# Recall in transposed layout, exp of phi from the copy on chip, and a newly searched plan, in a gated mix of attention with memory and a gated feed-forward layer

## The chip, the cores and the metric

The kernel runs on one core of one Trainium2 chip. The metric is device time in microseconds (us); lower is better. Every number of a run below is of a run in the fast state (one core, granted TensorE clock 0.993 to 1.000). The engines are called as the profile calls them: PE multiplies matrices, PEld loads its weights, DVE is the vector engine, ACT computes activations, POOL masks the attention here, and SP issues DMAs.

## The reference, cut to what matters

```python
def _A_ref(x, wq, wk, wv, wo, beta):         # S = 2048, D = 512, H = 32, Dh = 16, N = 4 segments of L = 512
    ...
    for s in range(N):
        qs, ks, vs = q[:, :, s], k[:, :, s], v[:, :, s]
        p = softmax(qs ks^T * scale + causal mask)
        a_dot = p vs
        pq = phi(qs)                          # phi(t) = t + 1 where t > 0, else exp(t)
        num = pq M                            # per head: 16 x 16 memory
        den = (pq z) + 1e-06
        o = g * num / den + (1 - g) * a_dot   # g = sigmoid(beta), one per head
        pk = phi(ks)
        M = M + pk^T vs
        z = z + sum(pk)
    return concat(o) @ wo

def _B_ref(x, W_gate, W_up, W_down):          # F = 1792
    gate = x @ W_gate
    return (relu(gate) * (x @ W_up)) @ W_down

x = A_x
g = sigmoid((x * gate_w).sum(-1))             # one per token
return g * _A_ref(x, ...) + (1 - g) * _B_ref(x, ...)
```

`pq M / den`, for all segments but the first, is called the recall.

## The kernel before

The kernel does not write its instructions in a fixed order. It describes tasks, each with an engine, an assumed duration, dependencies, a priority (`key`) and the PSUM banks and buffers that it needs, and then plays them through a list scheduler (`Plan`) while the program is built. The order in which tasks start in that play is the order of the program. A table `SHIFT` moves the priority of single tasks by their number; it is the result of a search. On the chip each engine keeps to its list: in the traces of the kernels before and after, the instructions of PE, DVE and ACT (2246 matmuls, 407 and 174 instructions in the changed kernel) start in exactly the program's order, compared by source line. A task may be marked `lock`: DVE and POOL tasks so marked are never planned at the same time.

```python
SHIFT = { 22: -80000, 23: 130000, ... }      # cut: 141 entries
...
    for t in sorted(ready, key=rank):        # in Plan.run
        ...
        if t.lock and busy["lock"] > now:
            continue
```

PSUM is the memory that matmuls write to. The plan divides it into eight banks; a fill of attention scores takes four, always the same, and the matmuls of everything else take whichever bank is free. Projections of Q and K land in a bank that two engines read, DVE for the copy in bf16 and ACT for the exp of phi:

```python
    def phi_exp(key, sl, a):
        es = plan.one("ex1")
        return es, plan.add("ACT", 478, key + 500, lambda: nc.scalar.activation(
            ex1[es.i][:], bank(sl), ACT.Exp), [a], ACL, need=[es], frees=[sl])
    ...  # proj_q: DVE casts bank(sl) to QT (frees=[sl] too); phi_exp(key, sl, a); DVE: pqT = phi(QT, ex1)
```

The recall puts heads in rows for the division: two matmuls per unit of eight heads, two banks, each flipped by DVE transposes into T (128x512 f32), then reciprocal, scaling and product there, and the product is flipped back with the attention result:

```python
    def recall(seg, c):
        for r in range(2):
            sl = work()
            a = plan.add("PE", 216, key + r, lambda r=r, sl=sl: nc.tensor.matmul(
                bank(sl), lhsT=mbd[i][:, c, r].rearrange("p j e -> p (j e)"), rhs=pqT[u % RQ][:],
                start=True, stop=True), [...], PEL, need=[sl])
            groups.append((sl, a))
        recalled[u] = normalise(u, 1, key, groups)   # 2 transposes, add, reciprocal, 2 products
```

The softmax here doesn't subtract the row's maximum and nothing guards it: scores larger than these inputs give would overflow.

## Time and profile before

277.18 us, median of three runs (277.01 to 277.35).

The head of the profile page: the span, each engine's busy time with its share and instruction count, and for PE and DVE the busy share in tenths of 40 equal slices.

```profile
span 275.4 us, 5541 instructions
PE 268.0 (97%) x2211; PEld 112.9 (41%) x2211; DVE 208.5 (76%) x457; ACT 195.5 (71%) x175; POOL 86.7 (31%) x139
PE   8999999989999999999999999999999999999995
DVE  5789788999999898598967992977998575464312
```

PE is busy everywhere. Because matmuls overlap (the profile gives each 128x512 one 380 ns), I also looked at starts: in an unbroken row, 128x512 matmuls start 216 ns apart. I call a hole whatever a start is later than is usual for its pair of shapes by over 0.12 us.

What the change touches, as groups of instructions (shape, count | busy us, mean ns of one | idle time just before them, and what ended it):

```profile
L657 DVE STREAM_TRANSPOSE T<-ps 128x512 f32<-128x512 f32 x56 | 37.1, 693 | 4.8 <-PE ps L626 4.3 <-PE ps L687 0.5
L511 ACT ACTIVATE ex<-ps 128x512 bf16<-128x512 f32 x24 | 14.3, 605 | 11.0 <-DVE ktr L538 8.9 <-DVE QT L522 1.2 <-PE ps L463 0.9
L687 PE MATMUL ps<-pqT,mbd 128*128 128x512 bf16 x24 | 8.1, 380 | 0.7 <-ACT ex L511 0.4
```

In the trace the two reads never overlap: of the 24 exps none runs at the same time as the cast of its bank, 18 come after it, and where one follows the other most closely the gap is 0.03 us. The casts in turn waited 1.1 us for exps. Why the two reads are kept apart, the trace doesn't show. One place where it costs PE something, from the chain of waits (start, length, what; all us):

```profile
92.66 0.65 DVE ktr L538
93.39 0.61 ACT ex L511
94.04 2.10 PE ps L463 x9
```

Cast, then exp, then the bank is free and PE goes on: the bank was held for 1.3 us from the start of the cast.

### The profile page before, as it was taken

The page shows a single profiled execution, that of the slowest core. Times are in us where ns is not written, and L with a number is a line of the kernel's source. Part 1 is how long each engine was busy: PE and PEld are TensorE (multiplying, and loading weights), DVE is VectorE, ACT ScalarE, POOL GpSimd, SP SyncE. Part 2 cuts the span into 40 slices and gives each one's busy share as a digit, 9 for nine tenths or more (in the row PEclk, how much of TensorE's full clock was granted, in tenths as well). Part 3 has the DMA queues.
Part 4 walks back from the last instruction along what each step waited for, and adds up shares of the span by engine and source line. Part 5 has one row for each costly group of instructions (what it writes and reads, how often), then busy time and mean ns, then how long its engine had stood idle before and what let it go on. Part 6 is the DMA issues. An engine that isn't in the chain of part 4 may idle for free.

```text
span 275.4 us, 5541 instructions
## 1 busy us (share of the span) xinstructions
PE 268.0 (97%) x2211; PEld 112.9 (41%) x2211; DVE 208.5 (76%) x457; ACT 195.5 (71%) x175; POOL 86.7 (31%) x139
## 2 busy tenths in 40 slices
PE   8999999989999999999999999999999999999995
PEld 4344344443434343433434444434343434444444
DVE  5789788999999898598967992977998575464312
ACT  2189899988887777988978779789878769333000
POOL 5023333324344253324242425243334342300000
PEclk9999999999999999999999999999999999999999
DMA  7999964022111120000000100000000010000011
GB/s 232 320 261 347 275 104 126 5 40 59 37 23 38 23 40 21 2 0 19 4 0 21 40 21 0 21 0 2 0 4 0 19 35 6 21 0 0 2 38 38
DMA packets 27993, 15.46 MB, mean 56 GB/s; under 512 B 15680, under 2 KB 27968, under 8 KB 27968
## 3 DMA queue, kind: packets, MB, share of 16 engines
q1 hardware_dynamic: 26752, 14.06, 19.7%
q10 hardware_dynamic: 1216, 1.06, 1.1%
q8 instruction: 17, 0.28, 0.5%
q14 instruction: 8, 0.07, 0.1%
HBM read 9.86 MB, written 2.10 MB: 43 GB/s over the span
## 4 chain that ended last, share of the span: by engine, by line
PE 84%; DVE 7%; ACT 4%; issue 2%; DMA 2%; SPq 0%; DVEq 0%; ACTq 0%
PE ps L463 65%; PE ps L584 8%; PE ps L626 7%; PE ps L687 2%; ACT ex L511 2%; ACT E L604 1%; DVE ktr L538 1%; PE ps L785 1%; ACT rgr L743 1%; DVE hT L749 1%; DMA ratio<-rcol 1%; DVE QT L522 1%; PE ps L480 1%; DVE pkT L506 1%; DMA rq<-ratio 1%
## 5 line engine op out<-in xcount | busy, mean ns | idle before, releaser
L604 ACT ACTIVATE E<-ps 128x2048 bf16<-128x2048 f32 x80 | 150.5, 1881 | 31.9 <-PE ps L584 26.2
L613 POOL TENSOR_SCALAR_AFFINE_SELECT E<-E 128x512 bf16<-128x512 bf16 x128 | 83.1, 664 | 150.8 <-ACT E L604 150.8
L463 PE MATMUL ps<-xT,wg_sb 128*128 128x512 bf16 x224 | 57.6, 380 | 0.1
L463 PE MATMUL ps<-xT,wu_sb 128*128 128x512 bf16 x224 | 57.2, 380 | 0.0
L463 PE MATMUL ps<-wd_sb,hT 128*128 128x512 bf16 (+1 forms) x238 | 54.5, 367 | 0.4 <-ACT ex L511 0.3
L749 DVE TENSOR_TENSOR hT<-ps,rgr 128x512 bf16<-128x512 f32 x56 | 37.8, 680 | 14.4 <-PE ps L463 9.3
L743 ACT ACTIVATE rgr<-ps 128x512 bf16<-128x512 f32 x56 | 32.1, 599 | 14.1 <-PE ps L463 13.8
L657 DVE STREAM_TRANSPOSE T<-ps 128x512 f32<-128x512 f32 x56 | 37.1, 693 | 4.8 <-PE ps L626 4.3
L463 PEld LDWEIGHTS <-hT 128*128 128x128 bf16 x238 | 21.6, 98 | 25.5 <-issue 5.4
L463 PEld LDWEIGHTS <-wu_sb 128*128 128x128 bf16 x224 | 20.4, 98 | 26.1 <-issue 4.3
L463 PEld LDWEIGHTS <-wg_sb 128*128 128x128 bf16 x224 | 20.3, 98 | 26.1 <-issue 4.7
L771 DVE TENSOR_SCALAR osr<-ps,ngcol 128x512 bf16<-128x512 f32 (+1 forms) x17 | 12.2, 719 | 24.4 <-PE ps L463 24.4
L511 ACT ACTIVATE ex<-ps 128x512 bf16<-128x512 f32 x24 | 14.3, 605 | 11.0 <-DVE ktr L538 8.9
L626 PE MATMUL ps<-E,Vp 128*17 128x256 bf16 (+3 forms) x512 | 20.6, 300 | 0.7 <-DVE hT L749 0.7
L662 DVE TENSOR_TENSOR och<-T,cfr 128x512 bf16<-128x512 f32 x28 | 20.4, 736 | 0.3
L584 PE MATMUL ps<-QT,KTe 32*128 32x512 bf16 (+3 forms) x256 | 17.3, 302 | 0.4 <-ACT E L604 0.4
L463 PE MATMUL ps<-wv_sb,xT 128*128 128x512 bf16 x64 | 17.0, 380 | 0.6 <-DVE grc L449 0.6
L463 PE MATMUL ps<-xT,wk_sb 128*128 128x512 bf16 x64 | 17.4, 380 | 0.1
L584 PE MATMUL ps<-QT,KTo 32*128 32x512 bf16 (+3 forms) x256 | 17.1, 299 | 0.1
L463 PE MATMUL ps<-xT,wq_sb 128*128 128x512 bf16 x64 | 16.6, 382 | 0.0
L463 PE MATMUL ps<-wo_sb,oT 128*128 128x512 bf16 (+1 forms) x68 | 16.6, 367 | 0.0
L626 PEld LDWEIGHTS <-Vp 128*17 128x17 bf16 x512 | 10.8, 91 | 13.2 <-issue 3.8
(70 smaller groups left out, 190.1 us busy)
## 6 DMA issues: line engine op xcount, KB each, us to landing
out_dram<-osr SPq DMA_DIRECT2D x15, 128.0 KB, 1.7
wd_sb<-in_B_W_down_dram SPq DMA_DIRECT2D x2, 896.0 KB, 10.1
xn<-in_A_x_dram SPq DMA_DIRECT2D x3, 512.0 KB, 3.9
wg_sb<-in_B_W_gate_dram SPq DMA_DIRECT2D x2, 512.0 KB, 9.2
wu_sb<-in_B_W_up_dram SPq DMA_DIRECT2D x2, 512.0 KB, 9.4
wg_sb<-in_B_W_gate_dram SPq DMA_DIRECT2D x2, 384.0 KB, 4.7
wu_sb<-in_B_W_up_dram SPq DMA_DIRECT2D x2, 384.0 KB, 5.3
wk_sb<-in_A_wk_dram SPq DMA_DIRECT2D x1, 512.0 KB, 7.3
```

The source lines that it names most:

```text
L463: nc.tensor.matmul(bank(sl)[:, 0:width], lhsT=lhsT, rhs=rhs, start=(start and q == 0), stop=(stop and q == n - 1))
L511: return es, plan.add("ACT", 478, key + 500, lambda: nc.scalar.activation(ex1[es.i][:], bank(sl), ACT.Exp), [a], ACL, need=[es], frees=[sl])
L584: nc.tensor.matmul(ps[:, j * L + off:j * L + off + n], lhsT=kt[32 * j:32 * j + 32, kb * P:(kb + 1) * P], rhs=QT[i][32 * j:32 * j + 32, kb ...
L604: nc.scalar.activation(Ef[:, e0 * L:e1 * L], ps[:, e0 * L:e1 * L], ACT.Exp, scale=SCALE),
L613: nc.gpsimd.affine_select(out=m, in_=m, compare_op=ALU.is_ge, fill=0.0, base=0, pattern=[[0, 4], [1, P]], channel_multiplier=-1)
L626: nc.tensor.matmul(bank(sl)[32 * j:32 * j + HW, kb * P:kb * P + w], lhsT=Vp[i][:, kb, 8 * c + 2 * j + r, 0:HW], rhs=E[(NFILL * u + f) % RE ...
L657: done.append(plan.add("DVE", 633, key - RL, lambda r=r, sl=sl: nc.vector.transpose(T[ts.i][:, r], bank(sl)), [a] + done, 60 if r else 0, ...
L662: nc.vector.tensor_tensor(och[ds.i].rearrange("p (q r e) -> p r q e", r=2, e=DH), t()[:, :, :, 0:DH], cfr[cs.i][:, :, :, None].to_broadcas ...
L687: a = plan.add("PE", 216, key + r, lambda r=r, sl=sl: nc.tensor.matmul(bank(sl), lhsT=mbd[i][:, c, r].rearrange("p j e -> p (j e)"), rhs=p ...
L743: r = plan.add("ACT", 478, key - RL, lambda sl=gsl, rs=rs: nc.scalar.activation(rgr[rs.i][:], bank(sl), ACT.Relu), [g], ACL, frees=[gsl])
L749: nc.vector.tensor_tensor(hT[hs1.i][:], bank(sl), rgr[rs.i][:], ALU.mult)),
L771: b = plan.add("DVE", 95 + 1.12 * w, key - RL, lambda: nc.vector.tensor_scalar(osr[os.i][:, 0:w], bank(sl)[:, 0:w], ngcol[:, tt:tt + 1], N ...
```

## The change

Intent: less work on PE and DVE in the recall, PSUM banks free sooner, and a plan searched anew. Four parts:

1. The recall's matmul is one per unit, and its result is already in the transposed layout that the output projection needs. The coefficient 1/den, times the token's part of the gate, is made by six small matmul groups (`dens`), in a layout of heads and tokens. It is written to DRAM and read back broadcast to 16 partitions per head; one DVE product applies it. The head's gate goes into the memory matrix itself.
2. The exps of phi read the bf16 copy that DVE made, not PSUM; the bank is free after the one cast.
3. `xn` has one buffer, not two, so that the load for segment 1 leaves the prologue.
4. The plan has a new rule (`GUARD`) and a new `SHIFT` table.

```diff
+GUARD = 0.0
 SHIFT = {
-    22: -80000, 23: 130000, 38: 50000, ...
+    34: 106376, 36: 113032, 40: -114448, ...        (177 entries)
 }
@@ in Plan.run
-                    if t.lock and busy["lock"] > now:
+                    if t.lock and (busy["lock"] > now or t.eng != "POOL" and any(
+                            p.lock and p.eng == "POOL" and now < p.avail < now + t.dur + GUARD
+                            for p in ready)):
                         continue
@@ phi
-    def phi_exp(key, sl, a):
+    def phi_exp(key, src, a):
         es = plan.one("ex1")
         return es, plan.add("ACT", 478, key + 500, lambda: nc.scalar.activation(
-            ex1[es.i][:], bank(sl), ACT.Exp), [a], ACL, need=[es], frees=[sl])
+            ex1[es.i][:], src(), ACT.Exp), [a], ACL, need=[es])
...
-            es, b = phi_exp(key, sl, a)
+            es, b = phi_exp(key, lambda: QT[i][:], prj["q", seg, c])
@@ the denominators, two per segment
+    def dens(seg, half):
+        ...
+                    nc.tensor.matmul(
+                        bank(sl)[32 * t:32 * t + 32, 0:P],
+                        lhsT=zbd[i][:, c].rearrange("p a h -> p (a h)"),
+                        rhs=pqT[(4 * seg + c) % RQ][:, t * P:(t + 1) * P], ...)
+        ... DVE: dnr = bank + 1e-6; dnr = 1 / dnr; dnr = dnr * rr
+        att["coefs", seg, half] = plan.add("SP", 360, key, lambda: nc.sync.dma_start(
+            out=coefs[n].rearrange("h t p -> t h p"), in_=dn()), [a], 2200, frees=[ds])
@@ the recall
+        b = plan.add("SP", 360, key - 3000, lambda: nc.sync.dma_start(
+            out=cdr[cs.i][:], in_=coefs[n][8 * k:8 * k + 8].rearrange("h t p -> h (t p)")[:, None]
+            .to_broadcast([8, 16, L])), [att["coefs", seg, c // 2]], 3800, need=[cs])
+        a = plan.add("PE", 216, key, lambda: nc.tensor.matmul(
+            bank(sl), lhsT=mbd[i][:, c].rearrange("p j r e -> p (j r e)"), rhs=pqT[u % RQ][:], ...)
+        a = plan.add("DVE", 605, key - RL, lambda: nc.vector.tensor_tensor(
+            omr[om.i][:], bank(sl), cdr[cs.i][:], ALU.mult), [a, b], DVL, need=[om], frees=[sl, cs])
(cut: buffers, the gate ratio in two forms, the memory matrices, adding omr to oT)
```

The new rule holds a locked DVE task back if a locked POOL task would become ready before the DVE task ended.

## The prediction

> **What bounds the kernel now.** TensorE. The page gives PE 97% busy (268.0 of 275.4 us), DVE 76%, ACT 71%, POOL 31%, clock full throughout. Busy matmul time proves little because matmuls overlap, so I took start-to-start distances from the timeline: back-to-back 128x512 matmuls start every 216 ns. [...] Each excursion to the attention tilings costs about 96 ns going in and 101 ns coming out (312 and 317 instead of 216). Beyond this there are only 16 larger holes after the first 5 us, together about 4.5 us: 1.1 us near 57 us, 1.0 near 29, and small ones around the recall matmuls (79, 93, 122, 155, 196-197 us), together about 2.1 us. The last 30 us are an unbroken row of L463 matmuls. The chain of waits agrees: PE 84%.
>
> **What the change does.**
> - PE: recall goes from 24 full matmuls (L687) to 12: -12 x 0.216 = -2.6 us. The six denominators (eight column-tiled matmuls of 128 columns each) add about 0.12 us each (estimate from the PV matmuls), linked behind a PV and thus without another tiling switch: +0.7 us. Net -1.9 us, all on the critical engine.
> - DVE: 24 of the 56 transposes T (693 ns) go: -16.6 us; 12 of 28 products och (736 ns) become products PSUM x SBUF (about 690 ns, like hT): -0.6; 12 reciprocals (342), 12 cfr products (239), 12 adds (183): -9.2; the grc product is halved: -1.2. Added are six denominators of add, 128-column reciprocal and product, about 0.33 + 0.9 + 0.35 us (estimate from the 4, 8 and 32 column reciprocals: 178, 204, 342 ns): +9.5; zbd products: +1. DVE 208.5 -> about 191 us, off the critical path except where it delays a PSUM release.
> - ACT: the same exps, about 605 ns; they now start after the DVE cast, while the PSUM bank comes free after one reader instead of two. Recall needs one bank per unit instead of two.
> - DMA: per segment the gate ratio in two forms, per half the coefficients to DRAM and back as broadcast (12 x 256 KB). DMA is nearly idle after 40 us (share below 0.3), so only latency matters, 2 to 4 us per hop. The load of xn for segment 1 leaves the prologue.
>
> **How much lands.** The 1.9 us of PE work lands whole. Fewer PSUM banks held and 17 us less DVE work should take perhaps a third of the 4.5 us of holes; but the plan is newly searched, the DRAM round trip is a new serial path before each recall product, and holes of the prologue (DMA landing, grc) stay. I put -1.3 us on it.
>
> **Prediction.** 277.2 - 1.9 - 1.3 = 274.0 us, 8 in 10 between 271.6 and 276.6. Faster by over 2%: 0.12; within 2%: 0.85; slower by over 2%: 0.03.
>
> **What would show the steps right.** Recall has 12 matmuls; PE start-to-start stays 216 ns; DVE busy 188 to 195 us; 32 instead of 56 transposes T; ACT and POOL busy unchanged within 3 us; holes on PE 2.5 to 4 us in total; the last 30 us unchanged.
>
> **What would make it wrong.** (a) The coefficients come back late and PE's banks fill: PE waits for DVE omr or the SP queue stalls; slower. (b) The new order removes nearly all holes, or puts more PV and QK excursions next to each other and so saves switches: below 271.6. (c) The exps wait for the casts, ACT's in-order queue delays the attention exps, new holes appear before QK. (d) The order search traded the nominal run for robustness.

## More of the kernel before

All waits of PE in that run (who waited for whom: us in total, times, longest):

```profile
PE ps L785 <- DVE mcol_e L352: 1.3, 1, 1.3
PE ps L626 <- DVE hT L749: 0.7, 1, 0.7
PE ps L463 <- DVE grc L449: 0.6, 1, 0.6
PE ps L687 <- ACT ex L511: 0.4, 1, 0.4
PE ps L584 <- ACT E L604: 0.4, 2, 0.2
PE ps L463 <- ACT ex L511: 0.3, 1, 0.3
```

The first is the start of the program. The others make 2.4 us. (This view sees only idle time beyond the modelled end of a matmul, so it shows less than the distances of starts.)

## The result, and the profile after

283.97 us, median of four runs (283.30 to 285.64), against 277.2 us. The ratio of the fast runs is 1.0254, with a 95% interval of 1.0203 to 1.0304: slower by 2.5%, where I had given this 3 chances in 100. (Ratios here are the mean time of one kernel's fast runs over that of the kernel before in the same rounds on the same chip, so not quite the quotient of the medians. Between jobs, which ran on different chips, I compare ratios.)

The head of the page:

```profile
span 281.6 us, 5599 instructions
PE 267.8 (95%) x2247; PEld 111.3 (40%) x2247; DVE 192.2 (68%) x423; ACT 196.1 (70%) x175; POOL 84.0 (30%) x142
PE   7999979999978999999999999999999989699995
DVE  3888969898979683799793943598692637165323
```

DVE lost 16 us of work, as planned, and PE did not get longer in busy time; but PE's row has dents that it did not have before. The changed groups:

```profile
L683 DVE STREAM_TRANSPOSE T<-ps 128x512 f32<-128x512 f32 x32 | 21.2, 692 | 7.5 <-PE ps L651 7.2
L536 ACT ACTIVATE ex<-ktr 128x512 bf16<-128x512 bf16 x12 | 7.6, 635 | 11.9 <-DVE ktr L563 11.9
L738 PE MATMUL ps<-pqT,mbd 128*128 128x512 bf16 x12 | 4.4, 380 | 1.0 <-DVE omr L743 0.7
L722 DVE RECIPROCAL dnr<-dnr 128x128 f32<-128x128 f32 x6 | 5.7, 948 | 0.1
```

The work is what I had counted: 12 recall matmuls, 32 transposes, reciprocals of 948 ns. The longest waits of PE, the start of the program left out:

```profile
PE ps L609 <- ACT E L629: 2.1, 3, 1.4
PE ps L488 <- ACT E L629: 1.5, 1, 1.5
PE ps L488 <- DVE Vp L592: 1.5, 1, 1.5
...
PE ps L488 <- DVE T L683: 0.9, 2, 0.6
PE ps L488 <- DVE hT L808: 0.8, 1, 0.8
PE ps L738 <- DVE omr L743: 0.7, 1, 0.7
```

With the small ones that is 8.8 us against 2.4 before: 6.4 us more, and the span grew by 6.2. By distances of starts the holes are now 11.3 us against 4.6, and 8.9 of them lie in three places. Busy time of the engines there (window and its length; busy us and count of PE, PEld, DVE, ACT and POOL; then clock, DMA share and GB/s):

```profile
36.00:46.00 10.00, 7.96 (x74) 3.25 (x73) 7.72 (x18) 7.12 (x7) 3.53 (x5) 1.00 0.72 62
79.00:88.00 9.00, 6.30 (x65) 2.56 (x63) 6.89 (x18) 8.16 (x8) 3.95 (x5) 1.00 0.74 132
230.00:247.00 17.00, 13.94 (x112) 5.37 (x111) 6.98 (x12) 12.01 (x9) 6.15 (x10) 1.00 0.06 19
```

PE, the first figure after the length, is idle for 7.8 of these 36 us. The three places look different. The chain of waits at the second one runs through the new round trip:

```profile
76.34 2.45 DMA coefs<-dnr
78.80 0.60 SPq L735
79.45 5.34 DMA cdr<-coefs
84.89 0.14 DVE omr L743
```

At the first place DVE waited 2.1 us for the later load of `xn`; at the third, the first 0.9 us stand behind a recall product for which DVE sat idle 2.0 us (its coefficients' read had been issued 5.2 us before, and such a read took 5.34 us above), and the other 2.6 us are waits for exps of the attention (`E`) and for a product of the feed-forward layer. A reader of these lines alone would blame the new structure: the DRAM round trip, which took 8.5 us here from the first issue to the last landing where the plan reckons 6.7 (twice 360 ns of issue, 2200 and 3800 ns of latency), and the single buffer of `xn`. That was one theory. The rival was the plan's order: the same tasks, badly lined up.

### The profile page after: what moved, and what is told of

It is laid out like the page before. It is cut to its first block, busy times and chain, and to the rows that moved or that the text cites. A ratio compares the mean times of both kernels' runs of the same rounds, so it can differ in the third digit from the quotient of the medians.

```text
span 281.6 us, 5599 instructions
## 1 busy us (share of the span) xinstructions
PE 267.8 (95%) x2247; PEld 111.3 (40%) x2247; DVE 192.2 (68%) x423; ACT 196.1 (70%) x175; POOL 84.0 (30%) x142
## 4 chain that ended last, share of the span: by engine, by line
PE 78%; DMA 6%; DVE 6%; ACT 5%; issue 2%; POOL 0%; SPq 0%; ACTq 0%; DVEq 0%
PE ps L488 64%; PE ps L609 8%; PE ps L651 5%; ACT E L629 4%; DMA xn<-in_A_x_dram 2%; DMA cdr<-coefs 2%; DMA wq_sb<-in_A_wq_dram 2%; DVE T L683 1%; PE ps L738 1%; DMA coefs<-dnr 1%; ACT rgr L802 1%; DVE QT L547 1%; DVE oT L664 1%; DVE junk L434 0%; DVE hT L808 0%
## 5 line engine op out<-in xcount | busy, mean ns | idle before, releaser
L638 POOL TENSOR_SCALAR_AFFINE_SELECT E<-E 128x512 bf16<-128x512 bf16 x128 | 81.9, 657 | 162.0 <-ACT E L629 162.0
L488 PE MATMUL ps<-xT,wu_sb 128*128 128x512 bf16 x224 | 56.6, 380 | 2.0 <-ACT E L629 1.5
L683 DVE STREAM_TRANSPOSE T<-ps 128x512 f32<-128x512 f32 x32 | 21.2, 692 | 7.5 <-PE ps L651 7.2
L651 PE MATMUL ps<-E,Vp 128*17 128x256 bf16 (+3 forms) x512 | 21.7, 300 | 0.5 <-DVE omr L743 0.4
L536 ACT ACTIVATE ex<-ktr 128x512 bf16<-128x512 bf16 x12 | 7.6, 635 | 11.9 <-DVE ktr L563 11.9
L609 PEld LDWEIGHTS <-KTe 32*128 32x128 bf16 x256 | 5.3, 91 | 22.9 <-issue 22.5
```

What stands on the lines that cost most here:

```text
L488: nc.tensor.matmul(bank(sl)[:, 0:width], lhsT=lhsT, rhs=rhs, start=(start and q == 0), stop=(stop and q == n - 1))
L609: nc.tensor.matmul(ps[:, j * L + off:j * L + off + n], lhsT=kt[32 * j:32 * j + 32, kb * P:(kb + 1) * P], rhs=QT[i][32 * j:32 * j + 32, kb ...
L638: nc.gpsimd.affine_select(out=m, in_=m, compare_op=ALU.is_ge, fill=0.0, base=0, pattern=[[0, 4], [1, P]], channel_multiplier=-1)
L651: nc.tensor.matmul(bank(sl)[32 * j:32 * j + HW, kb * P:kb * P + w], lhsT=Vp[i][:, kb, 8 * c + 2 * j + r, 0:HW], rhs=E[(NFILL * u + f) % RE ...
L683: done.append(plan.add("DVE", 633, key - RL, lambda r=r, sl=sl: nc.vector.transpose(T[ts.i][:, r], bank(sl)), [a] + done, 75 if r else 0, ...
```

## The experiments

Theory A: the order lost it; the new table doesn't fit the new rule. Theory B: the new structure lost it. Each edit is against the changed kernel or the kernel before, as said. All results were correct. E1 to E4 ran on one chip, E5 to E8 on another, E9 and E10 on a third, E11 on a fourth, each beside the kernel before.

### E1, without the guard

```diff
-GUARD = 0.0
+GUARD = -1e9
```

> The changed kernel with one constant altered, GUARD = -1e9, so that the plan never holds a DVE instruction back for a coming POOL one; all instructions the same, only their order differs. Theory A (the order lost it: the table SHIFT does not fit the rule with the guard, the new structure itself is worth the 2 to 3 us I predicted): 272 to 276 us, holes on PE after 5 us at most 5 us in total. Theory B (the new structure lost it: DRAM round trip of the coefficients, one xn buffer, exps that wait for casts): stays above 281 us, holes of 10 us or more.

271.59 us (271.20 to 271.98), ratio 0.9784 (0.9770 to 0.9799). The same instructions in another order are 12 us faster than the changed kernel and 2.2% faster than the kernel before. Theory B falls. What is left of PE's waits:

```profile
PE ps L488 <- issue: 2.2, 14, 0.2
PE ps L844 <- DVE mcol_e L362: 1.3, 1, 1.3
PE ps L488 <- DVE mzacc L773: 0.2, 1, 0.2
PE ps L738 <- DVE ktr L563: 0.2, 1, 0.2
```

The row "issue" is no wait: this trace has 2212 of 2247 matmul records, and a missing one leaves a gap of about a fifth of a microsecond. So PE has 0.4 us of waits after the start. The three windows of above, for comparison:

```profile
36.00:46.00 10.00, 9.79 (x88) 3.98 (x89) 9.20 (x22) 9.57 (x10) 4.69 (x6) 1.00 0.59 72
79.00:88.00 9.00, 8.79 (x78) 3.70 (x79) 7.83 (x18) 7.20 (x6) 3.06 (x5) 1.00 0.18 46
230.00:247.00 17.00, 16.68 (x111) 7.52 (x112) 9.06 (x16) 5.70 (x8) 2.45 (x4) 1.00 0.03 9
```

The DRAM round trip is still late in this run, and later than in the changed kernel. Who ended the idle time of the recall's product on DVE (us, times):

```profile
  DMA cdr<-coefs: 6.7, 5
```

DVE sits idle for 6.7 us on it, and PE hardly notices, with 0.4 us of waits in all: it has other matmuls to run. In the changed kernel the same wait was 1.9 us, and stood in the chain.

### E2 and E3, without the table, with and without the guard

```diff
-SHIFT = {
-    34: 106376, ... 1353: 29837,
-}
+SHIFT = {}
```

E3 also has `GUARD = -1e9`.

> The changed kernel with an empty SHIFT table and the guard kept. Theory A: the table and the guard do not fit each other, so that without the table, too, it is clearly below the changed kernel: 274 to 278 us. Theory B: 281 us or more. Theory C (the guard alone is bad whatever the table): 281 us or more here and 272 to 276 in e1_noguard.

> The changed kernel with an empty SHIFT table and without the guard: the fourth corner. Theory A: 275 to 279 us, a little slower than e1_noguard since nothing was searched. Theory B: 281 us or more. If it is faster than e1_noguard the table is bad by itself.

E2: 272.61 us (271.91 to 273.97), ratio 0.9827 (0.9796 to 0.9857). E3: 272.41 us (272.20 to 272.92), ratio 0.9816 (0.9802 to 0.9831). With the changed kernel and E1 that is a square:

| new structure | table | no table |
|---|---|---|
| guard | 283.97 | 272.61 |
| no guard | 271.59 | 272.41 |

(The first figure is from another job and chip than the other three; its ratio to the kernel before, 1.0254, against 0.9784, 0.9827 and 0.9816 says the same.)

Neither the guard nor the table is bad. Only the two together are. Both runs came out below the ranges that I expected, by 1.4 and 2.6 us: the structure is worth more than I thought.

### E4, the kernel before without its table

```diff
-SHIFT = { 22: -80000, ... }
+SHIFT = {}
```

> The kernel before with an empty SHIFT table: the unsearched order of the old structure, to be compared with e3_neither, the unsearched order of the new one (neither has the guard). Theory A: 278 to 281 us, so that e3_neither is 1.5 to 3 us faster at equal effort of search. Theory B: about 277 to 280 us and faster than e3_neither.

278.43 us (278.28 to 278.69), ratio 1.0030. At equal effort of search, none, the new structure is 6.0 us faster (272.41 against 278.43). I had predicted 1.9 us for the work on PE and 1.3 for holes. Two questions follow: how the table and guard collide (E5), and where the other 4 us come from (E6 to E11).

### E5, one entry less

```diff
-..., 752: 229700, 753: -104580, 755: -97169, ...
+..., 752: 229700, 755: -97169, ...
```

Guard and the other 176 entries stay. Task 753 is the first half of the V projection of segment 2, tile 2; the entry moves it forward.

> The changed kernel, guard and table kept, with one of the 177 entries of the table taken out: that of task 753, the first two matmuls of the V projection of segment 2, tile 2, which the table moves forward by 104580. Theory A (the order alone; one priority that the guard lets win at the wrong moment, 71 us, sends the plan down a bad path): 271.5 to 275 us. Theory B' (the guard with this table is bad in many places, and one entry cures little): 280 us or more.

273.67 us (272.37 to 275.74), ratio 0.9892 (0.9850 to 0.9933). One entry is worth 10 us, though not any entry: of the 177 this is one of the two whose removal the planner rates best. How I read it: the greedy scheduler sets off on another path from one decision on, and the entries were chosen for the decisions of one path. That the entries were chosen so is argued, not shown. The planner says the same when one lets it run by itself; these are its own estimates, worked out while the program is built, and no chip times. It puts the end of the kernel before at 271.7 us, of the changed kernel at 279.4, of E1 at 269.9, of E2 at 271.1. Of the 177 kernels that leave one entry out, with the guard, only 15 come below 273, and the middle one stays at 279.4; without the guard 135 of the 177 do, though the worst reaches 285.3. With this table every guard that was tried from -400 ns down gives the 269.9 of E1, and those from -300 to 20 ns give 272.7 to 279.6: the table fits a scheduler without the guard. In other words, the changed kernel's own plan already contained most of the loss, and the chip followed it: the span is 281.6 us. Only the first hole, where `xn` landed about 2 us later than planned, and the 0.9 us at 231 us are not in the plan.

### E6 and E7, where exps read from

E6 is E3 with the exps of phi on PSUM again; E7 is E4 with the exps on the copy. The edit of E6, cut to the Q half (E7 is its reverse in the old structure):

```diff
-            ex1[es.i][:], src(), ACT.Exp), [a], ACL, need=[es])
+            ex1[es.i][:], bank(sl), ACT.Exp), [a], ACL, need=[es], frees=[sl])
...
-            es, b = phi_exp(key, lambda: QT[i][:], prj["q", seg, c])
+            es, b = phi_exp(key, sl, a)
```

> As e3_neither (empty table, no guard, new structure, 272.4 us), but the exps of phi read PSUM again as before, and PSUM banks come free after two readers. Theory P (reading the copy matters, banks come free earlier): 274 us or more. Theory D (the shorter work on DVE makes nearly all of the structure's 6 us beyond PE's 1.9): 271.5 to 273.5 us.

> As e4_before_noshift (empty table, old recall, 278.4 us), but with the exps of phi reading the bf16 copy: that part of the change alone. Theory P: 276.5 us or less. Theory D: 277.5 to 279.5 us.

E6: 276.28 us (275.68 to 276.52), ratio 0.9957 (0.9940 to 0.9975). E7: 275.18 us (274.96 to 276.03), ratio 0.9927 (0.9907 to 0.9946). This is the second square, all without table and guard, as ratios to the kernel before:

| | exp from PSUM | exp from the copy | gain |
|---|---|---|---|
| old recall | 1.0030 | 0.9927 | 1.0% |
| new recall | 0.9957 | 0.9816 | 1.4% |
| gain | 0.7% | 1.1% | |

The few words about exp in the change's title are worth 2.9 to 3.9 us (1.03 and 1.41% of 277), somewhat more than the large rewrite of the recall (0.73 and 1.11%, or 2.0 to 3.1 us). My theory D, that it was DVE's load, falls, at least for this part. It isn't the exp itself, which is slower from the copy. The groups in E6, then in E3:

```profile
L509 ACT ACTIVATE ex<-ps 128x512 bf16<-128x512 f32 x24 | 14.2, 600 | 9.5 <-DVE ktr L536 6.1 <-DVE QT L520 3.2
```

```profile
L509 ACT ACTIVATE ex<-QT 128x512 bf16<-128x512 bf16 x12 | 7.6, 629 | 1.6 <-DVE QT L520 1.6
L509 ACT ACTIVATE ex<-ktr 128x512 bf16<-128x512 bf16 x12 | 7.5, 633 | 6.0 <-DVE ktr L536 5.9
```

630 ns from the copy, 600 from PSUM. The exp waits for the cast in both cases (9.3 us in E6, 7.5 in E3). What differs is PE: after the start, missing records aside, it has no wait in E3 and 3.5 us of them in E6, the largest of them not for the exps of phi but for what comes later in the chain, the attention's exps (`E`) and the recall's product:

```profile
PE ps L582 <- ACT E L602: 1.7, 5, 0.5
PE ps L461 <- DVE omr L716: 1.3, 1, 1.3
```

### E8, DVE's load alone

E3 with the DVE work of the old recall's transposes given back, into a tile that nobody reads (until they are done they also hold the buffer of the coefficients, `cdr`, a side effect that was not tested apart):

```diff
+        for _ in range(2):
+            plan.add("DVE", 633, key - RL, lambda: nc.vector.transpose(
+                tjunk[:], cdr[cs.i][:]), [a], DVL, frees=[cs])
         recalled[u] = a, om
```

> As e3_neither (272.4 us), with two more 128x512 f32 transposes of 128 partitions on DVE per recall unit, 24 in all, about 16.6 us of DVE work into a tile that nobody reads: the DVE load of the old recall without its PE work and PSUM banks. Theory D (DVE load makes the holes): 274 us or more, with the holes on PE back in the first 130 us. Theory P or another: below 273.3 us.

274.72 us (273.92 to 276.09), ratio 0.9910 (0.9878 to 0.9942), 0.9% more than E3 or about 2.6 us for 17 us of DVE work. So DVE's load does count, though it is not on the critical path by its share of the span. What I expected of the place was wrong: in the trace 2.9 us of new holes lie between 171 and 205 us, and little in the first 130. In the traced run, the slowest of the four, PE's only new wait of size is for a bank that DVE had yet to empty:

```profile
PE ps L461 <- DVE hT L785: 2.3, 3, 1.0
```

### E9 and E11, the wait or the bank

Why does reading PSUM cost so much? Either the plan doesn't know that exp and cast don't overlap, and lines tasks up wrongly, or the bank is held longer. E9 is E6 with the plan told; E11 is E3, exps on the copy, with the plan giving the bank away only after the exp.

```diff
 E9, against E6
-            es, b = phi_exp(key, sl, a)
+            es, b = phi_exp(key, sl, prj["q", seg, c])
 E11, against E3
-            ex1[es.i][:], src(), ACT.Exp), [a], ACL, need=[es])
+            ex1[es.i][:], src(), ACT.Exp), [a], ACL, need=[es], frees=[sl])
 (and the same for K)
```

> As e6_exp_psum (276.3 us: new structure, empty table, no guard, exps of phi from PSUM), but the plan is told that each exp starts only after the DVE cast of the same bank has ended; in e6_exp_psum the compiled program waits for that (ACT ex idle until DVE ktr and QT, 9.3 us) while the plan lets both start together. Theory S (the plan's ignorance of that wait makes the 3.9 us): at most 273.2 us. Theory H (the wait holds the PSUM bank by one more reader, known or not): 275.5 us or more. Between: both, in the share that the time shows.

> As e3_neither (272.4 us), exps of phi reading the copy, but the plan gives the PSUM bank of Q and K projections away only after the exp has ended too, as if it were a second reader. No instruction differs, only banks and order. Theory H (a bank held by one more reader costs the 3.9 us that e6 and e9 show): 275 us or more. Theory A' (it is ACT reading PSUM itself, or its wait, not the bank held): below 273.5 us.

E9: 276.20 us (275.09 to 277.16), ratio 0.9931 (0.9872 to 0.9989). E11: 275.66 us (275.13 to 275.81), ratio 0.9914 (0.9884 to 0.9944). Telling the plan brings next to nothing (0.9957 to 0.9931, intervals overlapping). The planner's own estimate explains how that can be: it reckons 271.1 us for E6 and 274.0 for E9, so what it gave away unknowingly in E6 it gives away knowingly in E9. All kernels bear this out: where the exps read PSUM and the plan doesn't know of the wait (before, E4, E6), the traced span is 3.6 to 3.7 us above the planner's estimate; in E1, E2, E3, E5, E7, E10 and E11 it is within 1 us of it. (E9 lies 1.2 above, E8 2.3, the changed kernel 2.2.) Holding the bank in the plan, with not one instruction changed, costs 1.0% over E3, about 2.7 us of the 3.9. A rival is that E11 met an unlucky order by chance. The planner alone speaks against it: over 200 small random changes of 60 priorities each, the middle half of its estimates is 271.4 to 271.9 us for E3 and 273.1 to 274.2 for E11. The programs of E9 and E11 have the same order on every engine; they differ in what ACT reads, and their times don't differ clearly. So most of the gain of reading the copy is the PSUM bank that comes free one reader, 0.6 us, earlier, 24 times. (In E11 only the plan holds the bank; in E6 the exp's read on the chip does, where ACT idled 9.3 us before exps until casts had ended, and in E9 both, with 6.0 us of such idle time. That the three losses are one and the same is inferred from their size.)

### E10, more work on PE

E3 with every recall matmul run twice into its bank, 2.6 us of PE work.

> As e3_neither (272.4 us), but each of the 12 recall matmuls is run twice into the same bank, 12 x 0.216 = 2.6 us more work on PE and nothing more on DVE. If PE work lands whole, as the prediction assumed: 274.6 to 275.4 us. If there is slack on PE that absorbs it: below 274 us.

275.00 us (274.72 to 275.36), ratio 0.9891 (0.9833 to 0.9948): 2.6 us more by the medians, 2.1 by the ratios. Work on PE lands whole or nearly so, as the prediction assumed. This trace has all its matmul records, and PE's only wait in it is the start of the program:

```profile
PE ps L820 <- DVE mcol_e L335: 1.3, 1, 1.3
```

By distances of starts it has 0.7 us of holes, against 4.6 in the kernel before.

The version that beats both kernels is E1: the changed kernel with the guard off, 271.59 us, 2.2% below the kernel before and 4.4% below the changed kernel by the medians.

## Why the prediction was wrong

**The step that failed** is the one under "How much lands": "Fewer PSUM banks held and 17 us less DVE work should take perhaps a third of the 4.5 us of holes; but the plan is newly searched ... I put -1.3 us on it." I took it for granted that a newly searched order would be at least as good as the old one. The holes grew from 4.6 to 11.3 us instead, as the table didn't fit the rule it was shipped with. E1, E2 and E5 show this: remove the rule, the table or one entry of 177 (this one, not any one), and 10 to 12 us are gone. The planner could have been asked beforehand: its estimates, 271.7 us before and 279.4 after, are 7.7 apart, and 6.8 were measured. Of my list of what might go wrong, (d) came nearest, but for a wrong reason: the square of E1 to E3 shows no price of robustness, only a mismatch. How the mismatch came about can't be seen from here, beyond the planner's hint under E5 that the table fits a scheduler without the guard.

**A second term was mis-sized**: what reading the copy brings. I wrote that it changes the 605 ns little, which is right (630), and that the bank comes free after one reader; but I put both this and DVE's relief into 1.3 us. E6 and E7 give 2.9 to 3.9 us for the copy alone, and E11 puts most of it down to the bank. I had counted on a third of the holes going; with an order that fits nearly all go (0.7 us left in E10). The sign was in the profile before: ACT's exp waiting 10.1 us for casts that it did not need. (A sign, not a measure: in E3 the exps, which now do need the casts, still wait 7.5 us for them.)

Point by point:

- *PE bounds the kernel, and its work lands whole.* Right (E10). Recall went to 12 matmuls, start to start stayed 216 ns, and the last 30 us stayed an unbroken row.
- *DVE falls to about 191 us, mostly off the critical path.* The size was right (192.2; reciprocal 948 ns against 0.9 us, product omr 687 ns against 690). "Off the critical path" was too strong: E8 puts about 2.6 us on 17 us of such work.
- *ACT and POOL busy unchanged within 3 us.* Right: 196.1 and 84.0 against 195.5 and 86.7.
- *2 to 4 us per DMA hop.* The write took 2.45 us; the broadcast read took 5.34, longer than predicted. (The 2 to 4 us were an estimate; in the profile before, small transfers land 1.9 (`rq`), 2.4 (`pK`) and 2.5 us (`ratio`) after issue at the median, and the 512 KB of `xn` 3.9.) It is late, but E1 shows that PE can do without it for 6.7 us.
- *Holes of 2.5 to 4 us.* Wrong with this order (11.3); right in direction with that of E1 (0.4 us of waits).
- *277.2 - 1.9 - 1.3 = 274.0.* The structure without any table gives 272.4; with a table that fits, 271.6, at the very edge of my range. That they come so close is partly luck, since the term for the holes was too small. My warning (b) describes E1, and the range missed on the side of the order.

What stays open: which of the guard's single decisions leads the plan astray. As dropping one entry mends nearly all, no single hole, the one at the late `xn` included, can be called the cause by itself. E5's four runs also spread more (272.4 to 275.7) than those of E1, which I did not explain; the longest is also the one with the lowest granted clock, 0.993.

## What to carry to other kernels

A searched order belongs to the exact rule and durations it was searched with: after any change of the scheduler, run the old table, an empty table and the new table against each other before believing a difference in the kernel. A plan that is worked out at build time gives an estimate that costs no run: compare it before and after, and compare it with the span of the trace. When an instruction waits for another engine's read of the same PSUM bank (10.1 us of ACT's idle time before), count how long the bank is held (1.3 us in the chain shown): a copy read a second time can be worth more than the arithmetic saved elsewhere (2.9 to 3.9 us against 2.0 to 3.1 here). Sums of work on each engine, right to 1% for DVE here (191 us predicted, 192.2 measured), say nothing about the holes that the order leaves on the bounding one.

## What single things cost here

- A second reader on 24 PSUM banks cost 1.0 to 1.4% (2.9 to 3.9 us of 277), and holding the bank in the plan without that read 1.0% over E3.
- The exp of 128x512 took about 30 ns more from the bf16 copy than from PSUM (630 against 600 ns).
- The reciprocal took 178, 344 and 948 ns for 4, 32 and 128 f32 elements per partition, which is 6.3 ns for each further element ((948 - 344) / 96), about six times as long as for a further element between two products of f32 inputs (`dnr` 270 ns for 128, `omr`, which reads PSUM and writes bf16, 687 for 512: 1.1 ns each).
- Between a 128x512 matmul and a 512-column one of the attention scores, starts are 312 ns apart going in and 317 coming out, instead of 216: 96 and 101 ns more. A matmul of the denominators starts 45 ns after the 128-column PV matmul that it follows, about as the next PV does (47 ns).
- One priority of 177, among the two best to drop by the planner's estimate, was worth 10 us of 284 here.
